# Counting out-of-range weights during the last feed-forward steps instead of after them, with the branch that uses the count in its default layout

## The chip, the cores and the metric

The kernel runs on one core of one Trainium2 chip. The metric is the device time in microseconds of one execution. A core has a matrix engine (PE, whose weight loads are listed apart as PEld), a vector engine (DVE), a scalar engine (ACT), GpSimd (POOL) and SyncE (SP), which starts the transfers here. A name with a q behind it (PEq, PEldq, SPq) stands for the sequencer of that engine: waits on semaphores, register loads, branches and the starting of transfers are done there.

## The reference, cut to what matters

```python
def _attn_ref(r, k, v, w, u):                    # 4 batches, 8 heads, 768 steps, head size 48
    state = zeros(B, H, D, D)
    for t in range(S):
        cur = einsum('bhd,bhe->bhde', u * k[t], v[t])
        y[:, :, t] = einsum('bhd,bhde->bhe', r[t], state + cur)
        state = w[..., None] * state + einsum('bhd,bhe->bhde', k[t], v[t])

def _moe_ref(x, w_in, w_out):                    # 3072 tokens, 384 -> 2048 -> 384
    h = x @ w_in
    sp = maximum(h, 0) + log1p(exp(-abs(h)))
    return (h * erf(sp)) @ w_out
```

The attention's output, with the heads side by side, is the input x of the feed-forward part. All arrays are 32-bit floats. The weights `w` are decays, one for each head and channel.

## The kernel before, in words

The sequence is cut into chunks of 128 steps, one chunk for each batch at a time, so that four chunks make a block of 512 tokens. There are six blocks. For each block the feed-forward part has 16 steps, one for each 128 of the 2048 hidden channels, 96 steps in all, numbered 0 to 95. A step n is made of these words: `f` (nine matmuls on PE that make the hidden tile `h`, L405), `a` and `b` (ACT, L412 and L416), `z` (DVE, L421), `c`, `d`, `e` (ACT, L425, L429, L433), `g` (DVE, L437), `h` (ACT, a rounded copy `gh`, L443), `l` (DVE or POOL, the rest `gl`, L448) and `p` (nine matmuls on PE, L464, that add into three accumulators). The step `p` can be split into `px`, `py` and `pz`, three matmuls for each accumulator; the second of each three reads `gl`. `O950`, `O951` and `O952` end the last block: part `a` copies an accumulator out of PSUM (ACT, DVE, and for the last one two half copies on ACT, L487), part `b` starts the transfer to the output (SP, L476, and two halves on L474).

The whole program but its end is written out by hand: `ORDER` is a list of words, and each engine gets its instructions in the order of this list. Nothing is moved by a scheduler. The string is run through by the loop that starts at L520.

The chunked form of the attention is used with the decays clipped to the range from 0.7 to 0.97. Whether any weight was clipped is found by `count_bad`, the word `Z0`, which is the last word of the list. It makes `bad` on DVE (L510, a comparison of 112 by 4 elements), multiplies it by a column of ones on PE (`cnt`, L512, two passes), takes the maximum on DVE (`fi`, L513), and loads this one number into a register of each of the five engines (`values_load`, L514). On SP, two more sequencer instructions behind the load check its bounds.

Behind the list stands `tc.If(rv > 0)` (L596). Its body computes everything again by a slower route that works for any decay. With the data of this case the count is zero and the body isn't run. The body is long: some 400 instructions on DVE, over 900 matrix instructions on PE, some 140 on ACT, some 70 on SP and some 50 on POOL. Where it isn't run, each engine executes a short block instead (the false block), which waits for the engine's own earlier work (on SP: eight waits, one for each semaphore of the transfers) and raises the semaphores to where the body would have left them. Behind both comes the end block (listed under L822): SP waits for everything once more, in eight waits, all engines meet, and the span ends.

The order in memory before the change is: program, false block, body, end block. An engine that doesn't run the body goes on from the branch into the false block, and then jumps over the body into the end block. So each engine has two branch instructions on its way.

Of the kernel before, what the change touches and what calls it, by code (L numbers as in the profile page):

```python
# [30 lines left out]
PR = 112  # L31
# [10 lines left out]
def body(ctx: ExitStack, tc: tile.TileContext, att, early, wcol, u, win, wout, levels, outT):  # L42
    nc = tc.nc
# [38 lines left out]
    def load_u():  # L82
        nc.sync.dma_start(out=ub, in_=u)
# [116 lines left out]
    def across(down):  # L200
        for hh in range(2):
            tp = ps1.tile([P, NPAIR, D], F32, tag=f"A{hh}", name="tp")
            r = slice(64 * hh, 64 * hh + D)
            for p in range(NPAIR):
                for c0 in (0, H):
                    jc = abs(c0 - H * ((hh + p) % 2))
                    nc.tensor.matmul(out=tp[jc:jc + H, p, :], lhsT=down[r, p, c0:c0 + H], rhs=ident[r, 0, r],
                                     start=True, stop=True)
            nc.scalar.copy(out=wkn[:, :, hh], in_=tp)
# [26 lines left out]
    def sum_b(g, tag):  # L236
        qp = bank(tag, [P, 2, P], f"qp{g}")
        for p in range(NPAIR):
            nc.tensor.matmul(out=qp[32 * p:32 * p + 32, 0, :], lhsT=uq[:, p, :], rhs=st_[g]["e"][:, p * C:(p + 1) * C],
                             start=True, stop=True)  # L240
        st_[g]["qp"] = qp

    def copy_rows(g, eng):
        o = st_[g]["qs"] = chunks[g][:, R0:R0 + P]
        (nc.scalar.copy if eng is nc.scalar else nc.vector.tensor_copy)(out=o, in_=st_[g]["qp"][:, 0, :])

    def turn_q(g):
        nc.tensor.transpose(out=st_[g]["qp"][:, 1, :], in_=st_[g]["qs"], identity=ident[:, 0])

    def copy_q(g, eng):  # L250
        q = a2.tile([P, NPAIR, 2], F32, tag="q", name=f"q{g}")
        i = st_[g]["qp"][:, 1, :].rearrange("p (a c) -> p a c", c=32)[:, :, 0:2]
        (nc.scalar.copy if eng is nc.scalar else nc.vector.tensor_copy)(out=q, in_=i)
        return q

    def turn_k(g):
        tp = bank("h" if g < 4 else "A1", [P, NPAIR, PR], f"kt{g}")
        for p in range(NPAIR):
            nc.tensor.transpose(out=tp[:, p, :], in_=chunks[g][:PR, 512 + p * C:512 + (p + 1) * C],
                                identity=ident[:PR, 0, :PR])  # L260
        st_.setdefault(g, {})["kt"] = tp

    def copy_k(g):
        o = chunks[g][:, K0:R0].rearrange("p (a b d) -> p a b d", b=2, d=D)
        for hh in range(2):
            nc.scalar.copy(out=o[:, :, hh], in_=st_[g]["kt"][:, :, 64 * hh:64 * hh + D])


    def diag_a(t, eng):
        eng.tensor_tensor(out=t[:, R0:AW], in0=t[:, R0:AW], in1=ub, op=ALU.mult)  # L270

    def diag_b(t, eng):
        eng.tensor_tensor(out=t[:, R0:AW], in0=t[:, R0:AW], in1=t[:, K0:R0], op=ALU.mult)

    def diag_c(t, g):
        q = a2.tile([P, NPAIR, 2], F32, tag="q", name=f"q{g}")
        nc.vector.tensor_reduce(out=q, in_=t[:, R0:AW].rearrange("p (a b d) -> p a b d", b=2, d=D), axis=AX.X,  # L277
                                op=ALU.add)
        return q
# [165 lines left out]
    def act_l(n, eng):  # L445
        e = ff[n]
        e["gl"] = fp.tile([P, TB], F32R, tag="gl", name=f"gl_{n}")
        eng.tensor_tensor(out=e["gl"], in0=e["s"], in1=e["gh"].bitcast(F32), op=ALU.subtract)  # L448
# [4 lines left out]
    def f2(n, part_e=None):  # L453
        b, f = order[n]
        first = n == 0 or order[n - 1][0] != b
        last = n + 1 == len(order) or order[n + 1][0] != b
        if first and part_e in (None, 0):
            for e in range(NQ):
                acc[e] = ps1.tile([P, TB], F32, tag=f"acc{e}", name=f"acc{n}_{e}")
        d = ff[n]  # L460
        for e in range(NQ) if part_e is None else (part_e,):
            es = slice(e * P, (e + 1) * P)
            for i, (w, g) in enumerate(((woh, d["gh"]), (woh, d["gl"]), (wol, d["gh"]))):
                nc.tensor.matmul(out=acc[e], lhsT=w[:, f, es], rhs=g,  # L464
                                 start=first and i == 0, stop=last and i == 2)
# [39 lines left out]
    fi = const.tile([1, 1], I32, name="fi")  # L505

    def count_bad():

        bad = const.tile([PR, NPAIR], F32, name="bad")
        nc.vector.tensor_tensor(out=bad, in0=wp[:, 0, 0], in1=wc, op=ALU.not_equal)  # L510
        cnt = ps1.tile([1, NPAIR], F32, tag="A0", name="cnt")
        nc.tensor.matmul(out=cnt, lhsT=mask[:PR, 0, P - 1:P], rhs=bad, start=True, stop=True)  # L512
        nc.vector.tensor_reduce(out=fi, in_=cnt, axis=AX.X, op=ALU.max)  # L513
        return nc.values_load(fi, min_val=0, max_val=PR)  # L514

    xp2 = []
    steps = dict(f=f1, a=act_a, b=act_b, z=act_z, c=act_c, d=act_d, e=act_e, g=act_g, h=act_h, p=f2)
# [2 lines left out]
    for i, x in enumerate(words):  # L520
        x, _, where = x.partition("@")
        eng = {"+": nc.gpsimd, "*": nc.scalar}.get(x[-1], nc.vector)
        what, x = x[0], x.rstrip("+*")
        num = int("".join(c for c in x if c.isdigit()))
        sub = x[-1]
        if what == "l":
            act_l(num, eng)
        elif what == "p" and sub in "xyz":
            f2(num, "xyz".index(sub))
        elif what in steps:  # L530
            steps[what](num)
        elif what == "N" and eng is nc.scalar:
            copy_k(num)
        elif what in preps:
            preps[what](num, eng)
        elif what == "L":
            (load_a if sub == "a" else load_b)(num)
        elif what == "U":
            load_u()
        elif what == "T":  # L540
            across(wk)
        elif what == "V":
            turn_k(num)
        elif what == "Z":
            rv = count_bad()
        elif what == "Q":
            st_.setdefault(num, {})
            if sub == "a":
                diag_a(chunks[num], eng)
            elif sub == "b":  # L550
                diag_b(chunks[num], eng)
            else:
                st_[num]["q"] = copy_q(num, eng) if num < 4 else diag_c(chunks[num], num)
        elif what == "B":
            sum_b(num, BANKS[where or "0"])
        elif what == "J":
            copy_rows(num, eng)
        elif what == "H":
            turn_q(num)
        elif what == "M":  # L560
            st_[num // 10]["am", num % 10] = diag_m(st_[num // 10]["q"], num // 10, num % 10, eng)
        elif what == "A":
            st_.setdefault(num, {})
            a_step(num, [BANKS[c] for c in where or "01"])
        elif what == "P":
            predicated(num // 10, st_[num // 10]["am", num % 10], st_[num // 10]["ap"][num % 10], mask.bitcast(U32), num % 10)
        elif what == "Y":
            y_step(num, BANKS[where] if where else f"acc{num % 2}" if num < 4 else "A0")
        elif what == "X":
            x_step(num, sub)  # L570
        elif what == "D":
            st_.setdefault(num, {})["ds"] = ds_product(chunks[num], BANKS[where] if where else "h" if num < 4 else "A1", f"ds{num}")
        elif what == "S":
            if sub in "ab":
                s_add(num, "ab".index(sub), eng)
            else:
                s_mul(num, "cd".index(sub), eng)
        elif what == "F":
            fetch_w(num // 10, num % 10)
        elif what == "C":  # L580
            load_w(sub, eng, num // 10, num % 10)
        elif what == "O":
            end(sub, num // 10, num % 10)
        elif what == "W":
            keep_warm(num)
        if i == last:
            late.close()
            xp2_pool = ExitStack()
            xp2.append(xp2_pool.enter_context(tc.tile_pool(name="xp2", bufs=1)))
# [3 lines left out]


    xp2_pool.close()
    with tc.If(rv > 0, preferred_fallthrough_block=False), tc.tile_pool(name="gen", bufs=1) as gen:  # L596
        lm = gen.tile([P, 3, 7, P], U32, name="lm")
        nc.sync.dma_start(out=lm, in_=levels)
        wpos, wrev = wr, wk
# [153 lines left out]
a86 h85 l84 b86 f87 l85+ z86 c86 p84 d86 e86 g86 p85 a87 b87 z87 c87 h86 d87 e87 l86+ g87 f88 f89 a88 O792b b88 z88  # L753
c88 d88 e88 f90 g88 h87 p86 a89 b89 l87 a90 h88 b90 z89 c89 d89 p87 e89 l88 g89 h89 z90 c90 d90 e90 l89 f91 a91 b91
f92 p88 a92 b92 g90 h90 z91 c91 d91 l90+ e91 z92 p89 g91 h91 f93 f94 c92 l91+ a93 b93 z93 d92 e92 p90 a94 c93 d93 e93
g92 h92 b94 f95 a95 b95 l92 z94 c94 p91 p92 g93 h93 l93 p93x z95 d94 p93y e94 c95 p93z g94 h94 l94 d95 e95 g95 h95
p94x p94y p94z l95 p95x O950a p95y O951a O950b O951b p95z O952a O952b Z0
"""


# [66 lines left out]
```

## Time and profile before

| | us |
|---|---|
| median of 3 runs | 510.5 |
| the runs | 510.13, 510.5, 511.52 |
| the profiled execution, whole time | 510.69 |
| its span, from the first to the last instruction | 508.9 |

The span is what the trace shows. It is 1.79 us shorter than the time of the same execution. Positions in the trace are in us from the start of the span, and all instruction times are given in us, where a row doesn't say ns.

### The profile page before, as it was taken

The page shows a single profiled execution, that of the slowest core. Times are in us where ns is not written, and L with a number is a line of the kernel's source. Part 1 is how long each engine was busy: PE and PEld are TensorE (multiplying, and loading weights), DVE is VectorE, ACT ScalarE, POOL GpSimd, SP SyncE. Part 2 cuts the span into 40 slices and gives each one's busy share as a digit, 9 for nine tenths or more (in the row PEclk, how much of TensorE's full clock was granted, in tenths as well). Part 3 has the DMA queues.
Part 4 walks back from the last instruction along what each step waited for, and adds up shares of the span by engine and source line. Part 5 has one row for each costly group of instructions (what it writes and reads, how often), then busy time and mean ns, then how long its engine had stood idle before and what let it go on. Part 6 is the DMA issues. An engine that isn't in the chain of part 4 may idle for free.

```text
span 508.9 us, 10505 instructions
## 1 busy us (share of the span) xinstructions
PE 493.1 (97%) x4176; PEld 389.5 (77%) x4176; DVE 338.1 (66%) x610; ACT 403.3 (79%) x747; POOL 183.1 (36%) x167
## 2 busy tenths in 40 slices
PE   7789999999999999999999999999999999999994
PEld 3567777877877777787878888787888888878883
DVE  7999999898876956765868644646556453353442
ACT  4788999999997666778776777878778777987982
POOL 6657335433265544625354033513312221202110
PEclk9999999999999999999999999999999999999998
DMA  8656343613605151250131350020120000000001
GB/s 309 222 215 247 123 154 125 216 62 116 243 23 182 64 166 50 90 190 13 51 134 43 105 190 0 7 87 1 63 91 0 1 2 0 33 31 1 0 1 68
DMA packets 14007, 47.34 MB, mean 93 GB/s; under 512 B 1664, under 2 KB 2560, under 8 KB 13952
## 3 DMA queue, kind: packets, MB, share of 16 engines
q1 hardware_dynamic: 13952, 46.61, 26.7%
q8 instruction: 35, 0.57, 0.5%
q14 instruction: 20, 0.16, 0.1%
HBM read 40.31 MB, written 6.29 MB: 92 GB/s over the span
## 4 chain that ended last, share of the span: by engine, by line
PE 86%; DVE 8%; ACT 2%; DMA 1%; issue 1%; POOL 1%; DVEq 0%; ACTq 0%; POOLq 0%
PE h L405 38%; PE acc L464 36%; PE y L339 6%; PE A L307 3%; PE ds L358 1%; DVE s L421 1%; DVE am L313 1%; DMA out_dram<-o 1%; DVE att L220 1%; DMA o<-part 1%; DVE wt L129 1%; DVE gl L448 1%; ACT gh L443 0%; DVE att L224 0%; DVE s L437 0%
## 5 line engine op out<-in xcount | busy, mean ns | idle before, releaser
L405 PE MATMUL h<-x,wih 128*128 128x512 f32 x576 | 183.1, 399 | 1.4 <-DVE s L437 1.0
L448 POOL TENSOR_TENSOR gl<-s,gh 128x512 fp32r<-128x512 f32 x52 | 69.0, 1328 | 213.9 <-ACT gh L443 186.6
L405 PEld LDWEIGHTS h<-x,wih 128*128 128x128 f32 x576 | 106.7, 188 | 28.3 <-DVE s L437 1.9
L464 PE MATMUL acc<-gh,woh 128*128 128x512 f32 x288 | 115.0, 399 | 0.0
L464 PE MATMUL acc<-gl,woh 128*128 128x512 f32 x288 | 114.1, 396 | 0.2 <-DVE gl L448 0.2
L405 PE MATMUL h<-x,wil 128*128 128x512 f32 x288 | 113.7, 395 | 0.0
L464 PE MATMUL acc<-gh,wol 128*128 128x512 f32 x288 | 113.7, 395 | 0.0
L437 DVE SCALAR_TENSOR_TENSOR s<-s,h 128x512 f32<-128x512 f32 x96 | 65.6, 685 | 61.4 <-ACT s L433 61.1
L421 DVE SCALAR_TENSOR_TENSOR s<-s,h 128x512 f32<-128x512 f32 x96 | 65.7, 686 | 59.3 <-ACT s L416 42.4
L425 ACT ACTIVATE s<-s 128x512 f32<-128x512 f32 x96 | 60.2, 628 | 37.3 <-DVE s L421 37.3
L443 ACT CAST gh<-s 128x512 fp32r<-128x512 f32 x96 | 58.7, 614 | 21.6 <-DVE s L437 16.0
L412 ACT ACTIVATE s<-h 128x512 f32<-128x512 f32 x96 | 56.7, 592 | 15.6 <-PE h L405 15.1
L464 PEld LDWEIGHTS acc<-gl,woh 128*128 128x128 f32 x288 | 54.2, 188 | 14.0 <-DVE gl L448 1.5
L464 PEld LDWEIGHTS acc<-gh,woh 128*128 128x128 f32 x288 | 54.1, 188 | 13.4 <-ACT gh L443 0.2
L405 PEld LDWEIGHTS h<-x,wil 128*128 128x128 f32 x288 | 54.1, 188 | 12.9
L464 PEld LDWEIGHTS acc<-gh,wol 128*128 128x128 f32 x288 | 54.2, 188 | 12.7
L416 ACT ACTIVATE s<-s 128x512 f32<-128x512 f32 x96 | 60.4, 632 | 2.1
L433 ACT ACTIVATE s<-s 128x512 f32<-128x512 f32 x96 | 60.3, 629 | 2.1
L429 ACT ACTIVATE s<-s 128x512 f32<-128x512 f32 x96 | 60.4, 629 | 1.9
L448 DVE TENSOR_TENSOR gl<-s,gh 128x512 fp32r<-128x512 f32 x44 | 31.6, 719 | 13.7 <-ACT gh L443 13.1
L290 POOL TENSOR_TENSOR am<-ident,q 128x512 f32<-128x512 f32 x17 | 19.0, 1118 | 25.9 <-DVE q L277 17.6
L339 PE MATMUL y<-am,att 128*32 128x128 f32 x768 | 25.5, 273 | 1.5 <-DVE am L313 1.3
(98 smaller groups left out, 514.0 us busy)
## 6 DMA issues: line engine op xcount, KB each, us to landing
att<-in_att_dram SPq DMA_DIRECT2D x24, 512.0 KB, 4.0
att<-in_att_dram SPq DMA_DIRECT2D x20, 608.0 KB, 5.6
raw<-in_win_dram SPq DMA_DIRECT2D x8, 768.0 KB, 6.4
raw<-in_wout_dram SPq DMA_DIRECT2D x8, 768.0 KB, 4.7
out_dram<-o SPq DMA_DIRECT2D x17, 256.0 KB, 2.2
part<-o SPq DMA_DIRECT2D x6, 256.0 KB, 3.8
o<-part SPq DMA_DIRECT2D x6, 256.0 KB, 4.2
att<-in_early_dram SPq DMA_DIRECT2D x4, 224.0 KB, 8.2
```

The lines of the kernel that those rows point to most:

```text
L339: nc.tensor.matmul(out=y[r:r + 32, q, :], lhsT=lhsT, rhs=rhs, start=r not in new, stop=True, skip_group_check=True)
L405: nc.tensor.matmul(out=h, lhsT=w[:, f, q, :], rhs=x[:, xi, q, :], start=k == 0, stop=k == 8)
L412: nc.scalar.activation(out=s1, in_=e["h"], func=AF.Tanh, bias=FB0, scale=FA0)
L416: nc.scalar.activation(out=s1, in_=s1, func=AF.Tanh, bias=FB1, scale=FA1)
L421: nc.vector.scalar_tensor_tensor(out=e["s"], in0=e["s1"], scalar=FG, in1=e["h"], op0=ALU.mult, op1=ALU.add)
L425: nc.scalar.activation(out=s, in_=s, func=AF.Tanh, bias=FB2, scale=FA2)
L429: nc.scalar.activation(out=s, in_=s, func=AF.Square, bias=FB3, scale=FA3)
L433: nc.scalar.activation(out=s, in_=s, func=AF.Square, bias=FB4, scale=FA4)
L437: nc.vector.scalar_tensor_tensor(out=s, in0=s, scalar=FC, in1=ff[n]["h"], op0=ALU.subtract, op1=ALU.mult, reverse0=True)
L443: nc.scalar.copy(out=e["gh"], in_=e["s"])
L448: eng.tensor_tensor(out=e["gl"], in0=e["s"], in1=e["gh"].bitcast(F32), op=ALU.subtract)
L464: nc.tensor.matmul(out=acc[e], lhsT=w[:, f, es], rhs=g, start=first and i == 0, stop=last and i == 2)
```

## The change

The word `Z0` is moved from the end of the list to the place between `l93` and `p93x`, three steps of the feed-forward part ahead of the end. It now makes the count only. The loads into registers are a word of their own, `G0`, which stands behind `p95z` (the last three matmuls) and before `O952a` and `O952b` (the last copies out of PSUM, and the last two transfers). The argument `preferred_fallthrough_block=False` of the branch is left out, so that it has its default layout.

```diff
@@ count_bad
         nc.tensor.matmul(out=cnt, lhsT=mask[:PR, 0, P - 1:P], rhs=bad, start=True, stop=True)
         nc.vector.tensor_reduce(out=fi, in_=cnt, axis=AX.X, op=ALU.max)
-        return nc.values_load(fi, min_val=0, max_val=PR)
@@ the loop over the words
         elif what == "Z":
-            rv = count_bad()
+            count_bad()
+        elif what == "G":
+            rv = nc.values_load(fi, min_val=0, max_val=PR)
@@ behind the list
-    with tc.If(rv > 0, preferred_fallthrough_block=False), tc.tile_pool(name="gen", bufs=1) as gen:
+    with tc.If(rv > 0), tc.tile_pool(name="gen", bufs=1) as gen:
@@ ORDER, its last two lines
-g92 h92 b94 f95 a95 b95 l92 z94 c94 p91 p92 g93 h93 l93 p93x z95 d94 p93y e94 c95 p93z g94 h94 l94 d95 e95 g95 h95
-p94x p94y p94z l95 p95x O950a p95y O951a O950b O951b p95z O952a O952b Z0
+g92 h92 b94 f95 a95 b95 l92 z94 c94 p91 p92 g93 h93 l93 Z0 p93x z95 d94 p93y e94 c95 p93z g94 h94 l94 d95 e95 g95 h95
+p94x p94y p94z l95 p95x O950a p95y O951a O950b O951b p95z G0 O952a O952b
```

## Rows read from the trace of the kernel before

**Rows 1.** The page: busy time of each engine, its share and instructions.

```profile
PE 493.1 (97%) x4176; PEld 389.5 (77%) x4176; DVE 338.1 (66%) x610; ACT 403.3 (79%) x747; POOL 183.1 (36%) x167
```

**Rows 2.** The branch's own instructions, L596: count, ns min/median/max, first and last start.

```profile
L596 SPq EVENT_SEMAPHORE  x8: 17/17/17, 505.4 to 505.9; - x8
...
L596 PEldq COMPARE_BRANCH  x2: 95/1892/3690, 504.1 to 504.4; - x2
L596 DVEq COMPARE_BRANCH  x2: 51/53/55, 504.1 to 504.3; - x2
L596 SPq COMPARE_BRANCH  x2: 43/46/49, 504.9 to 505.9; - x2
```

**Rows 3.** The end block, L822, same columns.

```profile
L822 SPq EVENT_SEMAPHORE  x10: 17/28/28, 506.4 to 508.9; - x10
...
L822 SPq DRAIN  x3: 7/7/7, 507.0 to 508.4; - x3
L822 DVEq DRAIN  x2: 10/34/57, 507.3 to 508.5; - x2
L822 PEldq DRAIN  x2: 8/40/73, 508.1 to 508.5; - x2
```

**Rows 4.** Transfers from 504.9 to 506 us: queue, packets, MB, share.

```profile
q8 instruction: 1, 0.02, 7.2%
```

**Rows 5.** The timeline of the last steps: start, length, instruction, idle before it.

```profile
494.26 0.69 DVE L448 TENSOR_TENSOR gl<-s,gh 128x512 fp32r<-128x512 f32 x1 [1.22 <-ACT gh L443]
...
494.98 0.69 DVE L421 SCALAR_TENSOR_TENSOR s<-s,h 128x512 f32<-128x512 f32 x1
...
495.51 0.39 PE L464 MATMUL acc<-gh,woh 128*128 128x512 f32 x1
...
497.75 0.19 PEld L464 LDWEIGHTS acc<-gl,woh 128*128 128x128 f32 x1 [0.19 <-DVE gl L448]
...
500.38 0.51 PE L464 MATMUL acc<-gl,woh 128*128 128x512 f32 x1 [0.23 <-DVE gl L448]
...
502.12 0.40 PE L464 MATMUL acc<-gh,wol 128*128 128x512 f32 x1
502.46 0.15 DVE L510 TENSOR_TENSOR bad<-wp,wu 112x4 f32<-112x4 f32 x1
...
502.76 0.19 PE L512 MATMUL cnt<-bad,mask 112*1 112x4 f32 x2 [0.24 <-DVE bad L510]
502.98 0.15 DVE L513 TENSOR_REDUCE fi<-cnt 1x1 int32<-1x4 f32 x1 [0.38 <-PE cnt L512]
```

**Rows 6.** The chain of waits over the same steps: start, length, what.

```profile
495.71 0.61 ACT s L425
...
500.38 2.15 PE acc L464 x8
```

**Rows 7.** SP's queue at the end, in the timeline.

```profile
501.77 1.13 SPq L476 DMA_DIRECT2D out_dram<-o  x2
502.99 0.90 SPq L474 DMA_DIRECT2D out_dram<-o  x2
```

**Rows 8.** The last two transfers, L474.

```profile
L474 SPq DMA_DIRECT2D out_dram<-o x2: 405/406/407, 503.0 to 503.5; - x2
...
DMA to landing us min/median/max: 1.9/1.9/2.0
```

**Rows 9.** The register loads, L514, same columns as L596.

```profile
L514 DVEq TENSOR_LOAD <-fi x1: 825/825/825, 503.2 to 503.2; - x1
L514 PEldq TENSOR_LOAD <-fi x1: 774/774/774, 503.2 to 503.2; - x1
L514 SPq TENSOR_LOAD <-fi x1: 617/617/617, 503.9 to 503.9; - x1
```

**Rows 10.** L307 (first matmuls of an attention chunk) from 315.3 to 321 us.

```profile
L307 PEld LDWEIGHTS A<-att x32: 129/133/135, 320.0 to 320.6; 48*64 48x64 f32 x32
...
L307 PEldq EVENT_SEMAPHORE  x2: 51/51/51, 315.7 to 315.8; - x2
```

## The prediction

> **What bounds the kernel now.** The page comes first [rows 1]: PE is busy for 97% of the span, so nearly all of the span is a row of matmuls, and the change doesn't touch their number. What it touches is the last stretch. The last matmul of the feed-forward part starts at 502.12 us and takes 0.40 [rows 5], so it ends at 502.5; I call that moment T. The span ends at 508.9. These 6.4 us behind T hold no large work, and the question is which engine is last in them. So I read the branch and the end block next.
>
> In the end block every engine meets the others with a DRAIN, and the last one to arrive lets the span end 0.8 us later [rows 3]. PE arrives at 508.1, DVE at 507.3, SP at 507.0. PE is last, though it has nothing to compute: its second branch starts at 504.4 and takes 3.69 us [rows 2], which ends at 508.05, and the DRAIN follows. DVE loses as much: its second branch starts at 504.3 and its DRAIN comes 3.0 us later [rows 2, 3]. SP makes the same jump at 505.9 and goes on at 506.4, for 0.5 [rows 2, 3]. While PE and DVE stand, instruction transfers run on queues of their own, one of them a packet of 0.02 MB [rows 4]. So I read the long branches as a jump to code that has to be fetched: the body is over 900 matrix instructions on PE and 400 instructions on DVE, but only some 70 on SP, which finds its target near.
>
> SP would be the next to end. Its end is made of the last transfer's landing, eight waits, the jump, and eight waits: 505.4, 505.9, 506.4, 507.0 [rows 2, 3]. In T: T + 2.9, T + 3.4, T + 3.9, T + 4.5. PE's arrival is T + 5.6.
>
> [...]
>
> **The count, moved.** It is two small DVE instructions with two PE passes between them, and this trip now stands in front of `z95` on DVE. `z95` starts at 494.98, as soon as `l93` (494.26, 0.69 long) ends [rows 5]. From there the chain of waits goes on without a gap over 0.1 us: `c95` on ACT at 495.71, and through `h94`, `d95`, `e95`, `g95`, `h95` and `l95` to the matmul of step 95 that reads `gl`, at 500.38, and from it through eight matmuls to T [rows 6]; that matmul even waits for `gl` [rows 5]. So all that delays `z95` delays T.
>
> How long? `bad` takes 0.15 [rows 5], so it is done at 495.1. PE takes its instructions in order: `cnt` comes behind step 92, where step 93 started before, 495.51 [rows 5]. The two passes take 0.19, to 495.70; the maximum starts 0.03 later (502.76 + 0.19 = 502.95 against 502.98), takes 0.15, and `z95` may begin at about 495.85 [rows 5]. That is 0.85 us late. The bounds: with PE free, the trip from the start of `bad` to the end of the maximum took 0.67 (502.46 to 503.13) [rows 5], from 494.95 to 495.6, so 0.6 late; and if `cnt` also had to wait for the last matmul of step 92 to drain, 0.40 more, so 1.25. I take 0.85, since the order on PE is fixed. PE's own 0.2 us for `cnt` costs nothing: step 94's `gl` came just in time before (its weight load at 497.75 waited 0.19 for it [rows 5]) and is late by the same 0.85 now, so PE has that long to spare. If that cover were gone, it would cost the 0.2. From step 94's `gl` to step 95's there is as much time as before, so no more is added: T moves to 503.4.
>
> **The loads, moved.** On PE the load (0.77) [rows 9] and the first branch stood behind the count, at 503.2. They now stand behind the last matmul in the queue, and PE's sequencer runs ahead of its matmuls: for an attention chunk it had done the waits at 315.7 whose matmuls began at 320.0, over 4 us later [rows 10]. So the load starts before T: about T - 1.9, when the wait for `gl` of step 95 is over (2.15 us before T [rows 6]) and the rest has been queued; without any run ahead, at T. Then 0.8, the branch, 3.7 and 0.2 for the false block and the DRAIN: PE arrives between T + 2.8 and T + 4.8, in place of T + 5.6. DVE's load (0.83) starts behind the issue of its last copy, before T; with 3.0 for the jump it arrives near T + 3.5, at most T + 4.2. ACT's and POOL's loads fall into waiting time for PE's last products; behind ACT's stand the last two half copies, but its load is done before T.
>
> On SP the move costs. `G0` stands in front of the last two transfers. Their predecessor is the second transfer of L476, which waits for the copy on DVE and is issued by 502.9, T + 0.4 [rows 7]. The load (0.62 [rows 9]) and the two bounds checks follow: before, from the end of the last issue, 503.9, to the branch, 504.9, they took 1.0 [rows 2, 7]. So the last two transfers start at T + 1.4 and T + 1.9 in place of T + 0.5 and T + 1.0 (405 and 407 ns each, and a wait between [rows 8]). The last lands 1.9 after its issue [rows 8], at T + 3.8.
>
> **The layout.** I take the default as program, body, false block, end block. The number of far jumps stays at one, but it moves from behind the false block to ahead of it. For SP that is worth the 0.5: the jump is now made at T + 2.4, while the last transfer flies, and the false block runs on into the end block. For PE and DVE the same fetch stands in the first branch. SP then: landing T + 3.8, eight waits 0.55, eight waits and a DRAIN 0.6, arrival T + 5.0. SP is the last engine, 0.2 behind PE's upper bound.
>
> **The sum**, against the profiled execution's span of 508.9 and time of 510.69: PE's arrival at T + 5.6 gives way to SP's at T + 5.0, which is -0.6; T moves by +0.85. Together +0.25: span 509.15, and with the 1.79 us outside the span 510.9. The profiled execution lies 0.2 above the median of the runs, 510.5, so the same step from the median gives 510.75. I write 510.9.
>
> **The rivals.** A difference under 0.3%, 1.5 us, can hardly be told from none in this kernel (its three runs lie 1.4 us apart).
>
> First, slower: SP's jump misses. At T + 2.4 SP goes over its body, and if the target isn't at hand it pays DVE's 3.0 in place of 0.5. Its 16 waits then start at T + 5.4, its arrival is T + 6.5, 1.5 later than in my sum: 512.4. It decides from the point where the miss ends after the landing, that is, at a miss over 1.4 us. For it: DVE and PE miss in this trace. Against it: SP's body is unchanged, and it jumped over it in 0.5 [rows 2, 3]. [...] Chance 0.06.
>
> Second, faster: the trip through PE is hidden, T stays, and SP's loads run beside its wait for the DVE copy. Then SP ends at T + 4.0, -1.6: 509.1. For it: sequencers do run ahead [rows 10]. Against it: the issue of the transfer before it waits on the same queue, and `z95` has no slack. Chance 0.06; T alone unmoved gives 510.1, which is within 0.3%.
>
> Third, the layout does nothing: the default is the old order. Then SP's jump stays behind the landing, +0.5: 511.4. Chance 0.1, within 0.3%.
>
> My forecast has 0.7, and cases between (0.6 or 1.25 for the trip, half of the loads hidden) 0.08. That leaves 0.83 within 0.3%; with the scatter of the runs I give slower 0.1 and faster 0.07. The bounds of the terms add up to 509.6 (0.6 for the trip, SP's loads hidden) and 511.8 (1.25, old layout); the scatter of the runs widens the upper side. I give 509.7 to 512.0.
>
> **What the next profile would show.** `bad`, `cnt` and the maximum lie near 495, `z95` starts near 495.85 and not at 495.0, and the last matmul ends near 503.4. PE's load starts before its last matmul ends; the long branch of PE is its first, and PE's DRAIN is before SP's. The last two transfers are issued 1.4 and 1.9 behind T, and SP's waits of the false block and of the end block follow each other without the half microsecond. I am wrong if `z95` is not late, if PE is still last, or if SP's branch takes over a microsecond.

## The result, and the profile after

The changed kernel takes 513.55 us (median of 4 runs, 512.84 to 514.42), the kernel before 510.31 (510.0 to 511.52, 4 runs). The ratio is 1.0057, with a 95% interval from 1.0040 to 1.0073: slower, by about 3 us. Forecast were 510.9 and no measurable difference; the range ended at 512.0.

The profiled execution of the changed kernel has a span of 511.5 us (508.9 before). The page's busy times first. They answer to [rows 1]: the same instructions in about the same time on every engine, with PE 2.5 us up. Of the 2.6 us between the two spans, 1.2 lie ahead of the end of the last matmul (T, 503.7 against 502.5) and 1.4 behind it.

```profile
PE 495.6 (97%) x4176; PEld 390.5 (76%) x4176; DVE 338.0 (66%) x610; ACT 403.1 (79%) x747; POOL 182.5 (36%) x167
```

The timeline of the last steps answers to [rows 5] (start, length, instruction, idle time before it).

```profile
495.16 0.15 DVE L510 TENSOR_TENSOR bad<-wp,wu 112x4 f32<-112x4 f32 x1
495.88 0.19 PE L512 MATMUL cnt<-bad,mask 112*1 112x4 f32 x2
496.11 0.15 DVE L513 TENSOR_REDUCE fi<-cnt 1x1 int32<-1x4 f32 x1 [0.80 <-PE cnt L512]
496.19 0.67 DVE L421 SCALAR_TENSOR_TENSOR s<-s,h 128x512 f32<-128x512 f32 x1
...
503.31 0.40 PE L464 MATMUL acc<-gh,wol 128*128 128x512 f32 x1
```

DVE stands for 0.80 us until PE has made `cnt`. `z95` starts at 496.19. The last matmul ends at 503.7, which is T of this execution. Now the branch and the end block, which answer to [rows 2, 3].

```profile
L597 SPq EVENT_SEMAPHORE  x8: 17/17/17, 509.6 to 510.2; - x8
...
L597 PEldq COMPARE_BRANCH  x1: 3522/3522/3522, 502.2 to 502.2; - x1
...
L597 SPq COMPARE_BRANCH  x1: 45/45/45, 506.4 to 506.4; - x1
```

```profile
L823 SPq EVENT_SEMAPHORE  x10: 17/28/28, 510.2 to 511.5; - x10
...
L823 SPq DRAIN  x3: 7/7/7, 510.8 to 511.1; - x3
...
L823 PEldq DRAIN  x2: 8/8/8, 505.9 to 511.1; - x2
L823 DVEq DRAIN  x2: 10/14/17, 506.7 to 511.1; - x2
```

PE makes its long jump at 502.2, ahead of the end of its matmuls, and is done at 505.9, DVE at 506.7. SP is last, at 510.8, as forecast, but at T + 7.1 and not at T + 5.0. Between its branch at 506.4 and its first wait at 509.6 lie 3.2 us. The SP queue and the last two transfers (L474) say why; they answer to [rows 7, 8].

```profile
502.95 1.59 SPq L476 DMA_DIRECT2D out_dram<-o  x2
505.51 0.81 SPq L474 DMA_DIRECT2D out_dram<-o  x2
```

```profile
L474 SPq DMA_DIRECT2D out_dram<-o x2: 332/358/383, 505.5 to 505.9; - x2
...
DMA to landing us min/median/max: 3.7/3.7/3.8
```

The last transfers land 3.7 us after their issue, where it was 1.9. The last one was issued at 505.9, lands at 509.6, and SP's first wait ends at 509.6. So SP waits for a transfer there; whether its jump was long can't be seen behind it. The stretch from 507.9 to 509.7 us shows what was still under way (the busy share of the 16 transfer engines in 40 slices, in tenths, and what they moved).

```profile
DMA  0001001001010101000000010000000000000000
GB/s 0 0 0 23 0 0 23 0 0 23 0 23 0 23 0 23 0 0 23 23 23 23 23 46 23 23 23 0 0 0 0 0 0 0 0 0 0 0 0 0
DMA packets 18, 0.02 MB, mean 9 GB/s; under 512 B 2, under 2 KB 18, under 8 KB 18
```

Only 18 packets move in 1.8 us, one after the other: 16 of 1 KB and two small ones. In this trace the last two transfers, of 128 KB each, make 256 packets of 1 KB, and the last four together have 64 small ones, 16 each. A sixteenth of the last two is 16 packets of 1 KB and two small ones, so I take the 18 as the share of one of the 16 engines; the trace names no engine. No other packet of the output moves behind 507.4. Ahead of the 18, from 506.3 to 507.7, stands this:

```profile
q8 instruction: 1, 0.02, 7.7%
```

7.7% of 16 engines' 1.4 us is 1.7 us of one engine, for one instruction packet on the queue q8, by which PE's code comes (e12 and e13 below show that). In the trace this packet starts at 506.37 and ends at 508.09; no output packet moves between 507.4 and 508.07, when the first of the 18 does. Whether PE's fetches are the cause was tried by the runs e12 and e13 (tails of 5.7 and 7.9).

The tail, from T to the end of the span, is the clean measure here. T itself lay anywhere between 502.5 and 506.6 us in the profiles, with the same program ahead of the last steps; from `z95` to T it was 7.5 us in every one of them. Part of that scatter stands already at the first feed-forward matmul, which began between 33.0 and 36.1 us. In this stretch PE's granted clock falls from 1.0 to 0.5 of full speed in some executions (in the changed kernel's profile for 3.4 us from 25.0) and not in others (the kernel before); how much of the scatter that makes isn't shown. In the changed kernel's profile, the row from 26 to 39 us (its length, PE's busy time and matmuls, mean granted clock, busy share of the transfer engines, GB/s) reads

```profile
26.00:39.00 13.00, 12.63 (x264) 0.91 0.57 215
```

where the kernel before had a clock of 1.00. So each run is judged by three distances in its trace, which is one execution, and by its ratio to the kernel before on the same chip, whose interval is wide.

| run | last transfer issued, behind T | landed after that | span ends behind T | ratio to before, 95% |
|---|---|---|---|---|
| before | 1.0 | 1.9 | 6.4 | |
| changed | 2.2 | 3.7 | 7.8 | 1.0057 (1.0040 to 1.0073) |
| changed again, e11 | 1.7 | 1.9 | 5.6 | 1.0026 (1.0005 to 1.0047) |
| changed again, e14 | 2.1 | 3.2 | 7.3 | |
| changed again, e15 | 2.2 | 3.3 | 7.4 | |
| e1 layout alone | 1.0 | 1.9 | 6.6 | 0.9990 (0.9967 to 1.0014) |
| e2 loads last | 2.0 | 3.7 | 7.6 | 1.0011 (0.9993 to 1.0029) |
| e3 old layout | 1.8 | 3.2 | 7.3 | 1.0056 (1.0036 to 1.0076) |
| e4 split | 2.2 | 3.3 | 7.4 | 1.0026 (1.0001 to 1.0051) |
| e5 small body | 1.8 | 1.8 | 5.5 | 0.9986 (0.9965 to 1.0008) |
| e6 before, small body | 1.0 | 1.9 | 5.2 | 0.9961 (0.9936 to 0.9986) |
| e7 PE late | 1.8 | 2.7 | 6.4 | 1.0027 (1.0003 to 1.0051) |
| e8 split, loads last | 1.7 | 3.6 | 7.2 | 1.0011 (0.9983 to 1.0038) |
| e9 split, loads last, PE late | 1.0 | 3.5 | 6.4 | 1.0007 (0.9989 to 1.0024) |
| e10 split, loads last, small body | 1.0 | 1.9 | 4.8 | 0.9952 (0.9930 to 0.9973) |
| e12 PE short, others long | 1.8 | 2.0 | 5.7 | 1.0007 (0.9981 to 1.0034) |
| e13 PE long, others short | 2.5 | 3.5 | 7.9 | 1.0021 (1.0003 to 1.0039) |

On the other chips the kernel before took 511.8 to 512.5 us, so the absolute times of the expectations, written against 510.3, are to be read as differences. The size of the loss is less sure than its sign: the result gives 2.9 us (2.0 to 3.7), the same kernel in e11 1.3 (0.3 to 2.4). In the traces the change costs 0.9 ahead of T (e4), and its tail is 7.8, 5.6, 7.3 and 7.4 against 6.4: 1.5 us together, in the mean of the four.

### The profile page after: what moved, and what is told of

Its sections match the earlier page's. It is cut to its first block, busy times and chain, and to the rows that moved or that the text cites. A ratio compares the mean times of both kernels' runs of the same rounds, so it can differ in the third digit from the quotient of the medians.

```text
span 511.5 us, 10500 instructions
## 1 busy us (share of the span) xinstructions
PE 495.6 (97%) x4176; PEld 390.5 (76%) x4176; DVE 338.0 (66%) x610; ACT 403.1 (79%) x747; POOL 182.5 (36%) x167
## 4 chain that ended last, share of the span: by engine, by line
PE 83%; DVE 8%; DMA 3%; ACT 2%; issue 2%; POOL 1%; SPq 0%; DVEq 0%; ACTq 0%; POOLq 0%
PE h L405 36%; PE acc L464 35%; PE y L339 6%; PE A L307 3%; PE ds L358 1%; DMA out_dram<-o 1%; DMA att<-in_att_dram 1%; DVE s L421 1%; DVE am L313 1%; DVE att L220 1%; DVE s L437 1%; DVE wt L129 1%; DMA o<-part 1%; POOL gl L448 1%; ACT s L425 0%
## 6 DMA issues: line engine op xcount, KB each, us to landing
att<-in_att_dram SPq DMA_DIRECT2D x24, 512.0 KB, 4.0
```

## The experiments

Three theories were tried. F: instruction fetches of the early far jump stand in the way of the last transfers. S: SP's own jump misses (the forecast's first rival). L: the last transfers are merely issued later.

**e1, the layout alone.** The kernel before, with one edit:

```diff
-    with tc.If(rv > 0, preferred_fallthrough_block=False), tc.tile_pool(...) as gen:
+    with tc.If(rv > 0), tc.tile_pool(...) as gen:
```

> The kernel before with the default layout alone; count and loads stay at the end. Theory F (fetch in the transfers' way): what costs 2.5 us in the changed kernel is that PE's and the other engines' instruction fetches for the far jump now run while the last transfers run, so that one share in 16 of each lands late. Here the loads are still behind the transfers, the first fetch comes at about 505.1 us of the span, when nearly all data of the transfers has moved, so nothing is late; SP's jump moves ahead of the landing. Time 510.0 to 510.6, the last landing 1.9 to 2.0 us after its issue. Theory S (SP's own jump misses when it is made by the conditional branch): SP's jump takes 3.3 us here too and the time is 511.4 to 511.8. Theory L (the late issue of the last transfers is all): the time is that of before, 510.3.

```profile
L596 SPq EVENT_SEMAPHORE  x8: 17/17/17, 505.8 to 506.3; - x8
...
L596 PEldq COMPARE_BRANCH  x1: 3978/3978/3978, 504.4 to 504.4; - x1
...
L596 SPq COMPARE_BRANCH  x1: 45/45/45, 505.3 to 505.3; - x1
```

SP jumps at 505.3 by the conditional branch and stands in the false block at 505.8. The last transfer, issued at 503.9, landed 1.9 after that, at 505.8 too. So the jump takes half a microsecond at most, and theory S is out: from the conditional branch it is 0.5 us here, from the jump behind the false block it was 0.5 in the kernel before [rows 2, 3]. The layout alone gains nothing, because PE is still last (its branch, 3.98 us from 504.4, ends at 508.4).

**e2, the loads behind the last transfers.**

```diff
-p94x p94y p94z l95 p95x O950a p95y O951a O950b O951b p95z G0 O952a O952b
+p94x p94y p94z l95 p95x O950a p95y O951a O950b O951b p95z O952a O952b G0
```

> The changed kernel with the loads behind the last two transfers in the list, which moves them on SP and ACT alone; PE's and DVE's loads, and their fetches, stay where they are. Theory F: the last two transfers are issued 1.0 us earlier and are nearly through when PE's second fetch starts (2.7 us behind the last matmul); landing 2.0 to 2.6 us after the issue in place of 3.7; time 510.5 to 511.2. Theory L: 1.0 us is gained and no more, 512.5. Theory S: the jump still takes 3.3 us, from 2.4 us behind the last matmul, so nothing is gained: 513.3.

```profile
L474 SPq DMA_DIRECT2D out_dram<-o x2: 602/622/641, 505.3 to 506.0; - x2
...
DMA to landing us min/median/max: 2.7/3.2/3.7
```

By its trace, no theory's number came. (Its time, 0.6 us over that of before with bounds of -0.4 and 1.5, is one that theory F allowed, 0.2 to 0.9; but the landing that theory F named, 2.0 to 2.6, didn't come.) The transfers were not issued 1.0 us earlier: SP's issue of `O951b`, of the first half and of the second half took 1.16, 0.60 and 0.64 us, against 0.33, 0.41 and 0.41 before, so the last one started 2.0 behind T. The share that was late landed 3.7 after that. The long first issue, from 0.06 behind T, stands beside PE's first packet, from 0.5 ahead of T to 0.85 behind it; whether the one held the other isn't shown, and in e11 an issue under such a packet took 0.33. The gain of the order alone was eaten by this.

**e3, the old layout put back.**

```diff
-    with tc.If(rv > 0), tc.tile_pool(...) as gen:
+    with tc.If(rv > 0, preferred_fallthrough_block=False), tc.tile_pool(...) as gen:
```

> The changed kernel with the old layout put back (false block in front of the body). PE now makes its far jump behind the false block's wait for its last matmul, so its first fetch comes about 1.7 us later than in the changed kernel and its second behind all transfers. Theory F: the first fetch can still meet the last transfers, the second can't; the last landing is 2 to 3 us after its issue; SP's jump comes behind the landing, 0.5 us; time 512.2 to 513.2. Theory S: SP's jump is short again, 3.3 us fall to 0.5: 512.2 or less with a landing of 3.7 us unchanged in the trace. Theory L: 514.0, 0.5 more than the changed kernel.

```profile
L474 SPq DMA_DIRECT2D out_dram<-o x2: 332/875/1418, 507.9 to 508.3; - x2
DMA to landing us min/median/max: 3.2/3.2/3.3
```

PE's far jump starts behind T here (T is 506.6, its long branch starts at 506.7), and its fetch falls on the last issue, which took 1.42 us in place of 0.41. The landing is 3.2 after the issue, a little over theory F's 2 to 3; the tail is 7.3. The layout isn't the cause: with the old one the moved loads cost as much. This run had the latest T of all (506.6; its granted clock was at half for 10.2 us near the start), so its ratio says less than its tail.

**e4, the maximum moved away from `z95`.** The comparison and the matmul stay, the maximum becomes a word of its own.

```diff
-l93 Z0 p93x z95 d94 p93y e94 c95 p93z g94 h94
+l93 Z0 p93x z95 d94 p93y e94 c95 p93z g94 I0 h94
```

> The changed kernel with the maximum (the second DVE instruction of the count) moved from in front of z95 to behind g94; the comparison and the matmul stay. If the trip from DVE to PE and back is what moves the last matmul, z95 follows l93 after 0.1 to 0.2 us, the last matmul ends 0.75 us earlier and the time is about 512.8. If PE's own work on the count moves it, nothing is gained: 513.5. Theories F, S and L say the same here: what stands behind the last matmul keeps its length.

```profile
494.74 0.69 DVE L448 TENSOR_TENSOR gl<-s,gh 128x512 fp32r<-128x512 f32 x1 [1.22 <-ACT gh L443]
495.35 0.15 DVE L512 TENSOR_TENSOR bad<-wp,wu 112x4 f32<-112x4 f32 x1
495.47 0.69 DVE L421 SCALAR_TENSOR_TENSOR s<-s,h 128x512 f32<-128x512 f32 x1
...
496.67 0.14 DVE L548 TENSOR_REDUCE fi<-cnt 1x1 int32<-1x4 f32 x1
```

From the start of `l93` to `z95` it is 0.73 us, the same as in the kernel before (494.26 to 494.98 [rows 5]). In the changed kernel it is 1.64. So the trip costs 0.91: 0.80 of it is DVE's wait for PE, the rest the maximum, and the comparison itself hides. The tail, 7.4, is that of the changed kernel. The gain is read from the trace alone: the time is 1.3 us over that of before (0.1 to 2.6; 2.5 was expected), and that of the changed kernel in e11 is 1.3 as well.

**e5 and e6, a short body.** The changed kernel and the kernel before, each with a body in which SP keeps its transfers, and so about its old length, and PE, ACT and DVE have next to nothing; the slower route, which isn't run with this data, is left out.

```diff
-        wpos, wrev = wr, wk
-        ...
-        with tc.For_i(0, NB, 1) as blk:
-            ...
+        o = gen.tile([P, TB], F32, name="go")
+        nc.vector.memset(o, 0.0)
+        with tc.For_i(0, NB, 1) as blk:
+            for b in range(4):
+                t = apool.tile([P, AW], F32, tag="att", name=f"gatt{b}")
+                nc.sync.dma_start(out=t, in_=...)
+                diag_a(t, nc.gpsimd)
+            for e in range(NQ):
+                nc.sync.dma_start(out=..., in_=o)
```

> The changed kernel with a short body of the branch: SP keeps its transfers there, GpSimd a few instructions, PE, ACT and DVE have next to nothing, so the slower route is left out (it isn't run with this data). No engine has to jump far. Theory F: no instruction fetch in the last 8 us, the last transfer lands 1.9 to 2.0 us after its issue in place of 3.7, and the time is about 511.8. Theory S: SP's jump over a body of about the old size still takes 3.3 us: 513.5. Theory L: 513.5.

> The kernel before with the same short body (the slower route is left out). If PE's far jump set the end of the kernel before, its DRAIN falls from 508.1 to about 504.5 us, SP's at 507.0 is last, and the time is 1.1 us under that of before: 509.2. If SP or the landing set it, the time stays at 510.3.

The changed kernel with the short body (e5), the last two transfers and the branch:

```profile
L474 SPq DMA_DIRECT2D out_dram<-o x2: 336/359/382, 504.4 to 504.8; - x2
...
DMA to landing us min/median/max: 1.7/1.8/1.8
```

```profile
L597 PEldq COMPARE_BRANCH  x1: 223/223/223, 501.5 to 501.5; - x1
```

PE's branch takes 0.22 us, the transfers land 1.8 after their issue, and the tail falls from 7.8 to 5.5. Theory L fell with it, since the issue is nearly as late as ever (1.8 behind T, against 1.7 to 2.2 in the changed kernel). The time came out lower than the 511.8 expected, which is 1.5 us over that of before: the ratio is 0.9986 (0.9965 to 1.0008). By the traces a trip of 0.9 and a tail that is 0.9 shorter cancel, which lies inside the interval. In the kernel before (e6), the tail falls from 6.4 to 5.2, by the 1.1 that lay between PE's and SP's arrival: PE's far jump did set the end of the kernel before, as read in the prediction.

**e7, PE held until the last matmul.**

```diff
         elif what == "G":
+            late_mm = ps1.tile([1, NPAIR], F32, tag="A0", name="late_mm")
+            nc.tensor.matmul(out=late_mm, lhsT=mask[:PR, 0, P - 1:P], rhs=outs[NS - 1, 1][:PR, 0:NPAIR], start=True, stop=True)
             rv = nc.values_load(fi, min_val=0, max_val=PR)
```

> The changed kernel with one more small matmul on PE between the last product and the loads, which reads what the last DVE copy wrote: it holds PE's load, and so its far jump, until the last matmul is done, 2.2 us later than in the changed kernel. Nothing else moves. Theory F: PE's first fetch then comes about 1.6 us behind the last matmul, before the last two transfers' data, and its second about 4.9 us behind, when they have landed; the last landing is 1.9 to 2.6 us after its issue, time 511.8 to 512.5. Theory S and theory L: no change, 513.5.

The landing is 2.7 after the issue and the tail 6.4, close to theory F's bound. The time was no better than that of the changed kernel in e11 (ratios 1.0027, 1.0003 to 1.0051, and 1.0026), so by its time alone this run decides nothing.

**e8 and e9, mends together.** e8 has the edits of e4 and e2, e9 those of e4, e2 and e7.

> Both mends together: the maximum behind g94, and the loads behind the last two transfers. Theory F: last matmul 0.75 us earlier than in the changed kernel, landing 2.0 to 2.6 us after the issue, time 509.7 to 510.4, at or a little under the kernel before. Theory L: 511.7. Theory S: 512.6.

> Three mends together: the maximum behind g94, the loads behind the last two transfers, and PE held by the small matmul that reads the last DVE copy. Theory F: PE's first fetch starts 1.9 us behind the last matmul, when the data of the four transfers (issued from 0.8 us ahead of it to 1.0 us behind it) is mostly through; the last landing is 2.9 to 3.7 us behind the last matmul, the span ends 5.3 to 5.9 us behind it (6.4 in the kernel before, 7.8 in the changed one), and the time is 0.5 to 1.1 us under that of before, which the runs can hardly tell. If the fetch did no harm in itself and only the order on SP did, the tail is that of the run with the two mends alone, 7.2.

Both fell short. In e8 the landing is 3.6 after the issue and the tail 7.2; in e9, with the last issue back at 1.0 behind T, the landing is still 3.5 after it, and the tail is 6.4, that of the kernel before (5.3 to 5.9 was expected). PE's fetch started 2.1 behind T and met the end of the transfers. Neither beats the kernel before.

**e10, both orders mended, and the short body** (edits of e4, e2 and e5; the slower route is left out).

> The maximum behind g94, the loads behind the last two transfers, and the short body of the branch (the slower route, which isn't run, is left out): no late z95, no loads in front of transfers on SP, no far jump. Theory F: the last landing is 2.8 to 2.9 us behind the last matmul, the span ends 4.7 to 4.9 us behind it, and the time is 1.5 us under that of before. This is what the change could bring if the jump cost nothing.

```profile
L474 SPq DMA_DIRECT2D out_dram<-o x2: 407/407/407, 504.6 to 505.1; - x2
...
DMA to landing us min/median/max: 1.9/1.9/2.0
```

The tail is 4.8, as expected, and the ratio 0.9952 (0.9930 to 0.9973). That is 1.6 us less than in the kernel before. But 1.1 of this is the short body alone, since the kernel before has a tail of 5.2 with it (e6); order and layout add 0.5, and the times of e10 and e6 (0.9952 and 0.9961) can't be told apart. By this reading, had the early fetch cost nothing, the order would have hidden PE's far jump and brought the 1.6 with the long body too; with it, the fetch takes this back (e8, e9).

**e11, e14 and e15, the changed kernel again.** No edit.

> The changed kernel once more, on another chip: a second trace of its end. Theory F: one of the 16 shares of the last transfer lands 1 to 2 us behind the other 15 again, the span ends 7 to 8 us behind the last matmul, the time is 2.0 to 3.3 us over that of before. If the late share was an accident of the one profiled execution, the span ends some 6 us behind the last matmul.

> The changed kernel, a third look at its end. Its first look had one share of the last transfer 1.9 us behind the others, its second look none. Theory F: PE's first fetch falls into the first two transfers every time, so one share of the transfer issued first is late by 0.5 us or more; whether the last one is late too hangs on where PE's second fetch falls, and the end lies between 5.5 and 8 us behind the last matmul.

> The changed kernel, a fourth look at its end; the same expectation as for the third. If the late share were tied to a place in the program and not to the moment of the fetch, its size would be that of the first look, 1.9 us.

In e11, against theory F's expectation, the late share is missing, and this profiled execution took 511.23 us, the fastest of its 12 (median 513.64, up to 515.99):

```profile
L474 SPq DMA_DIRECT2D out_dram<-o x2: 332/422/512, 505.2 to 505.6; - x2
DMA to landing us min/median/max: 1.9/2.0/2.0
```

PE's first fetch packet started 0.04 ahead of T there, and 0.6 ahead of it in the other three traces; its second came 3.2 behind T, and 2.6 to 2.7 in the other three, where the landing took 3.2 to 3.7. So half a microsecond in the fetch goes with 1.7 to 2.3 us at the end. In e14 and e15 the landing is 1.4 later than before, in the first trace 1.8: the lateness follows the moment of the fetch and not a place in the program. The tail without the collision, 5.6, is what the prediction's sum gave (T + 5.0 and 0.8 for the meeting of the engines).

**e12 and e13, whose fetches.** Bodies of filler, the slower route left out: e12 is long on DVE and ACT and short on PE, e13 long on PE alone.

```diff
# e12, in the short body of e5
+        for _ in range(400):
+            nc.vector.memset(o, 0.0)
+        for _ in range(140):
+            nc.scalar.copy(out=o2, in_=o)
# e13, in the short body of e5
+        for _ in range(300):
+            nc.tensor.matmul(out=pm, lhsT=mask[:PR, 0, P - 1:P], rhs=mask[:PR, 0, 0:NPAIR], start=True, stop=True)
```

> The changed kernel with a body that is short on PE and keeps its old length on DVE (some 400 instructions), ACT (some 140) and SP; the slower route is left out, these instructions only fill the place. PE's jump is near, DVE's is far. If PE's fetches (16 KB each) are what holds the late share, all 16 shares of the last transfer land within 0.1 to 0.4 us of each other, 1.8 to 2.2 us after the issue, and the span ends 5.5 to 5.8 us behind the last matmul. If the 8 KB fetches of DVE and ACT are enough, a share is late by 0.5 us or more.

> The changed kernel with a body that is long on PE (some 300 small matmuls that fill the place) and short on DVE and ACT, as on SP before; the slower route is left out. PE's jump alone is far. If PE's fetches are what holds the late share, a share of one of the last three transfers is late by 0.5 to 2 us and the span ends 5.6 to 7.8 us behind the last matmul, as the two fetches fall. If DVE's fetches do it, nothing is late and it ends 5.5 us behind it.

First e12, then e13:

```profile
L597 PEldq COMPARE_BRANCH  x1: 223/223/223, 502.3 to 502.3; - x1
L474 SPq DMA_DIRECT2D out_dram<-o x2: 333/500/667, 505.1 to 505.5; - x2
DMA to landing us min/median/max: 2.0/2.1/2.1
```

```profile
L597 PEldq COMPARE_BRANCH  x1: 3762/3762/3762, 502.6 to 502.6; - x1
L474 SPq DMA_DIRECT2D out_dram<-o x2: 332/357/382, 506.2 to 506.7; - x2
DMA to landing us min/median/max: 3.5/3.5/3.6
```

The instruction packets from 504 us on, again first e12, then e13 (queue, packets, MB, share):

```profile
q14 instruction: 4, 0.03, 1.7%
```

```profile
q8 instruction: 1, 0.02, 1.5%
q14 instruction: 1, 0.01, 0.4%
```

Where PE's body is short, nothing comes on q8 there. With PE's jump far and all others near, the tail is 7.9 (5.6 to 7.8 was expected), all of the loss; with DVE's and ACT's far and PE's near it is 5.7. The times alone don't tell the two apart (1.0021 and 1.0007, with intervals that overlap). But all 17 traces say the same. In ten of them a packet on q8 starts between 0.7 us ahead of the last issue and 1.2 behind it (1.5 in e2, whose issue was long), and the landing takes 2.7 to 3.7 us. In the seven others no packet comes on q8 at the end (e5, e6, e10, e12), or it starts 1.5 behind the last issue (e11) or later (e1 and the kernel before), and the landing takes 1.8 to 2.0. PE's fetches are the cause. (In e12 a transfer of 256 KB ahead of the last two took 3.1 us to land, where it was 2.0 in the kernel before, with four packets of 8 KB on q14 from 504 us on. It hides behind the last one.)

## Why the prediction was wrong

**What bounded the kernel before** was read rightly: PE's far jump, then SP (in e6, without the far jump, the tail is 5.2 in place of 6.4).

**The count's trip** was sized at 0.85 us and measured 0.91; all of it reached T, as the chain said. T moved by 1.2 between the two profiles; the other 0.3 stood ahead of `l93` already (494.55 against 494.26), from the scatter of the first stretch.

**PE's and DVE's loads** ran ahead as forecast, and somewhat further: PE's load started 2.1 ahead of T, PE arrived at T + 2.2 (forecast T + 2.8 to T + 4.8) and DVE at T + 3.0 (T + 3.5). Neither was last any more.

**The step that failed** is in the paragraph on SP: "The last lands 1.9 after its issue [rows 8], at T + 3.8." It measured 3.7, at T + 5.9. A smaller part failed in the same paragraph: the predecessor's issue took 0.79 and not 0.33, so the last issue came at T + 2.2 in place of T + 1.9. Together, 1.8 and 0.3, this is the 2.1 us between the tail that the sum gave, 5.8, and the 7.8 that came. Behind the first stands an omission. (The issue of 0.79 stood beside PE's first packet; why it was long isn't shown.) I had priced PE's fetch as time in which PE stands, and moved it ahead to where PE's standing is free. But a fetch is also a transfer: in the changed kernel's trace PE's two packets of 16 KB at the end took 1.1 us from 503.1 and 1.7 us from 506.4, and behind the second came the 18 late packets of the output. In the kernel before, the two came at 505.4 and 508.7, and the last packet of the output moved at 505.0 [the first of the two in rows 4, the landing of 1.9 in rows 8]. The change pulls them into it. PE itself loses 2 us at most by the fetches of the long stretch before: it is busy for 446 of the 448 us from 52 to 500, in which 27 packets come on q8. But beside the packet at 506.4 the last transfer landed 3.7 us after its issue in place of 1.9.

**The rivals.** The first came nearest to the time, with 512.4 against 513.55, but by the wrong cause: SP's jump is short (0.5 us at most in e1), and where the late share was absent SP's first wait ended with the landing, 1.9 after the issue (e11). The second and third can be closed: `z95` had no slack, and the default layout is the new order (PE has one branch instruction at L597, where it had two at L596). No rival named the fetch's own traffic. None of the three signs of being wrong appeared either: `z95` was late, PE wasn't last, and SP's branch took 45 ns. A late landing wasn't among them.

What stays open: how often the collision falls, since it turns on half a microsecond of the fetch; 3 of the 4 traces of the changed kernel had it. Which of the 16 engines carries PE's code wasn't tried, nor why some issues on SP get long.

## What to carry to other kernels

A step that is moved can bring transfers along. Here the far jump brought two instruction packets of 16 KB, and the last landing went from 1.9 to 3.7 us after its issue. So ask what else is on the transfer engines at the place it moves to, above all a transfer that the end waits for: here 18 late packets among the 576 of the last four transfers held SP until 509.6. Moving a wait off the last engine is worth only what the next one leaves; here the next was SP, 1.1 us ahead of PE, and the change had put work in front of SP's last transfers at the same time. A small instruction that needs another engine's answer should not stand in front of a chain without slack: with its second half moved back by two instructions of its engine, it cost nothing in the trace (e4: 0.73 us from `l93` to `z95`, where it was 1.64).

## What the hardware showed that I had not expected

- A far jump on PE took 3.4 to 4.0 us in all traces with the long body, 0.18 to 0.22 with a near target (e5, e6, e10, e12).
- Beside instruction packets, some of SP's issues of a transfer took 0.5 to 1.4 us (1.16 in e2, 1.42 in e3, 0.51 in e11); where no packet ran beside the last four issues (the kernel before, e1, e5, e6, e10), all took 0.33 to 0.41. Not each issue beside a packet is long: in e11 one took 0.33.
- PE's sequencer ran its load 2.1 us ahead of the last matmul's end, as soon as the weight load that waited for the last `gl` had started.
- With the same program, PE's granted clock dropped from 1.0 to 0.5 of full speed once within the first 34 us in 12 of 17 profiles, for 3.4 to 10.2 us, and not at all in the other 5. In e3, with 10.2 us of it, the first feed-forward matmul began at 36.1 us, in the kernel before, without it, at 33.0; but in e4 and e5, with 3.4 us of it, at 33.2.
